# Two routed expert layers behind a short convolution: the first epochs are cut 5 and 2 instead of 7, and the weight addresses of a step are made two to a chunk

## The chip, the cores and the metric

The kernel runs on one core of a Trainium2 chip. The metric is the device time of one execution in microseconds (us). Times of the kernel before are those of three runs and of one profiled execution.

## The reference, cut to what matters

The input x has 4 sequences of 3584 tokens with 192 channels, 14336 tokens in all. Three layers follow one another:

```python
# 1. causal depthwise convolution, 7 taps, softmax of the taps, 8 heads of 24 channels
out = np.einsum('hk,bskhg->bshg', softmax(weight), x_unfolded)
# 2. top-1 experts: 8 experts, 192 -> 1024 -> 192
expert = argmax(x @ w_gate);  p = softmax(x @ w_gate)[expert]
out[n] = p * (relu(x[n] @ w1[expert]) @ w2[expert])
# 3. noisy top-2 experts: 8 experts, 192 -> 1024 -> 192
noisy = x @ w_gate + log1p(exp(x @ w_noise)) * noise
top2 = the two largest of noisy;  q = softmax over the two
out[n] += q_k * (relu(x[n] @ w1[e_k]) @ w2[e_k])      # for both experts
```

## The kernel before

**Units and epochs.** The tokens come in 32 units of 448 (four tiles of 112). `tokens` carries one unit from its load to its scatter: convolution on TensorE (`ph<-x,band`), a split of each value into two halves of 16 bits, transposes, the gate's logits (`pl<-oneoa,rT`), the choice of the expert, a rank within the expert (`rank_mm`, `slots`), and four indirect DMAs from GpSimd (`rows<-row,di`) which put each token's row into the region of its expert in DRAM. `EPOCHS` cuts the 32 units into groups. When a group of units is counted, `epoch_tables` takes a snapshot of the experts' counters, and `table` works out from it, in a chain of small VectorE instructions, which full tiles of 512 or 256 tokens of one expert can be run; what is left goes to the next epoch. The last epoch also has tiles of 128, padded. A unit of epoch k may take its ranks only when k epochs are closed, so that the counters of a snapshot hold exactly the units of its epoch.

**The wait of the first snapshot.** `epoch_tables` begins with one loop that waits both for the counted units and for `ready[0] < 2`. `ready[0]` counts three preparations of the first expert layer's weights: the split of w1 (`first_w1`), the split of w2 (`first_w2`), and the products of w2 with the second gate (`gate_products`). The tables of all epochs go through one lane, one after another.

**Steps.** A tile of T tokens of one expert is a step. `load` reads the tile's place and its expert from the table with two `value_load`s on SyncE, fetches the expert's w1 (`w1t<-w1s`, 1 MB) and the rows, transposed (`xT<-rows`), and a small side table (`ax<-rows`). The DMAs on rows wait for the scatters in `g.deps`, which are all scatters recorded when the epoch was closed. `mm1` makes the hidden layer in 8 chunks of 128 hidden units. A chunk is five matmuls of T columns (`ph<-xT,w1t`); in large steps of the second layer it is four, and half of the small remainder is done for two chunks at once with 64 rows. `mm2` makes the output, three matmuls a chunk and 128 tokens (`py<-w2r,h`). `run` issues the chunks of mm1 of a step alternately with those of mm2 of the step before, so the step before is finished only when the next one has begun.

**Weight addresses.** w2 of all experts is resident in SBUF, and which expert a step uses is known only at run time. `addresses` therefore loads one offset from the table into a register of TensorE (`value_load`) and makes 16 addresses from it with 16 register additions. It is called once in a step, behind the second matmul of the first chunk. TensorE's instructions are read in order, so the matmuls behind it are read after the 16 additions. The four steps that bridge the two layers have w2 of their own (`st.g.own`) and need no addresses.

**Order.** Each engine's order of instructions is fixed when the program is built: a planner (`pump`, `live`, `clk`, `Queue`) runs all the generators against assumed costs and emits whichever instruction is due. The register instructions have no cost in it. `feed` starts the units, with a limit on how many may be under way.

**Two layers.** The first expert layer has 2 steps of 512 tokens, 45 of 256 and 21 of 128; the second has 4 bridge steps of 512, 45 further steps of 512, 7 of 256 and 21 of 128. Rows of the second layer's outputs are added to the result with indirect DMAs (`out_dram<-y,ax`).

Of the kernel before, what the change touches and what calls it, by code (L numbers as in the profile page):

```python
# [13 lines left out]
OP = mybir.AluOpType  # L14
# [5 lines left out]
N, D, E, F = 14336, 192, 8, 1024  # L20
FC = F // P
# [3 lines left out]
NT = SEQ // OT  # L25
G = 4
NG = NT // G
EPOCHS = (7, 4, 3, 4, 4, 4, 6)
DG = D + 2 * E
MAIN = 2 * D  # L30
HALF = MAIN // 2
# [10 lines left out]
NX, NROW, NRT = 4, 4, 3  # L42
# [5 lines left out]
W2_AT = 21472  # L48
# [6 lines left out]
def n_ceil(avail, t):  # L55
    return (avail + E * (t - 1)) // t
# [3 lines left out]
def conv_moe_moe2_kernel(ctx: ExitStack, tc: tile.TileContext, xh, cw, cwb, wg, w11, w21, w2t, w12, w22, out):  # L60
# [64 lines left out]
    v = Queue(nc.vector, "dve", 0.07, 1.04e-3)  # L125
# [11 lines left out]
    def vv():  # L137
        return on("dve", "dve", lat=0.06)

    def poll():  # L140
        return now[0] + 0.25, None

    def spawn(gen, rank=1, at=None):
        live.append([(now[0] if at is None else at, None), gen, rank])
# [196 lines left out]
    s1 = [cst.tile([P, E], F32, name=f"s1_{m}") for m in range(2)]  # L341
    s2 = [cst.tile([P, E], F32, name=f"s2_{m}") for m in range(2)]
    sE = [cst.tile([P, E], F32, name=f"sE_{m}") for m in range(2)]
# [137 lines left out]
    ready = [0, 0]  # L481
# [70 lines left out]
    def second_weights():  # L552
        while done[0] < sum(EPOCHS):
            yield poll()
        open_prep("prep2")
        spawn(second_w1(), 2)
        spawn(second_w2(), 2)
# [73 lines left out]
    def snapshot(m, tag):  # L631

        r = cst.tile([P, E], F32, name=tag + "snap")
        v.tensor_sub(r, cnt[m][cur[m]], reg_e)
        return r
# [99 lines left out]
    flying = [0, 0]  # L735
    done = [0, 0]
# [9 lines left out]

    def tokens(i, epoch):
        b, g = divmod(i, NG)
        wide = epoch == 0 and i % 2
        xs = "y" if wide else "x"  # L750
        yield from take(xs)
        rs = "row0" if wide else "row1"
# [113 lines left out]
    def feed():  # L866
        i = 0
        for k, n in enumerate(EPOCHS):
            for _ in range(n):
                while flying[0] >= (NROW if k else 7) or (k > 1 and ready[0] < 3) or (k and done[0] < EPOCHS[0]):  # L870
                    yield poll()
                flying[0] += 1
                spawn(tokens(i, k), 1 if k == 0 or ready[0] == 3 else 2)
                i += 1
                yield now[0] + 0.5, None

    def pad_rows(m, rows, total):
        pi = cst.tile([P, E], I32, name=f"pi{m}")
        v.scalar_tensor_tensor(pi, total, part, reg_e, op0=OP.add, op1=OP.add)
        yield on("pool", "dve")  # L880
        res = []
        for e in range(E):
            res.append(row_write(m, scatter(rows, pi[:, e:e + 1], pads)))
            yield on("pool")
        return res

    def epoch_tables(k, groups):
        while done[0] < sum(EPOCHS[:k + 1]) or ready[0] < 2:
            yield poll()
        if k == 0:  # L890
            v.tensor_mul(sE[0], s1[0], s2[0])
        total = snapshot(0, f"e{k}")
        closed[0] += 1
        deps = list(scat1)
        put = clk["put"]
        for g in groups:
            if g.last:
                deps = deps + (yield from pad_rows(0, rows1, total))
                put = clk["put"]
            g.deps, g.put = deps, put  # L900
            yield vv()
            yield from table(g, total)
# [34 lines left out]
    def mm1(st, f):  # L937


        T, n = st.T, 512 // st.T  # L940
        if f == 0:
            st.h = wk.tile([P, 2, 512 * FC // n], F16, name="h", tag="h", bufs=2)
            st.hv = st.h.rearrange("p k (c t) -> p k c t", c=FC)
        st.ph = [ps_h.tile([P, 512], F32, name="ph") for _ in range(st.nb)]
        x = lambda k: st.xT[:, k, :]

        def w(b, j, k):
            c = (f + b) * n + j
            return st.w[0][:, k * F + c * P:k * F + (c + 1) * P]

        out_ = lambda b, j: st.ph[b][:, j * T:(j + 1) * T]
        def whole(b):
            for j in range(n):
                o = out_(b, j)
                first = j == 0 and b < 2
                t_.matmul(o, w(b, j, 0), x(0), start=first, stop=False, skip_group_check=True)
                t_.matmul(o, w(b, j, 0), x(2), start=False, stop=False, skip_group_check=True)
                if f == b == j == 0 and not st.g.own:
                    addresses(st)
                t_.matmul(o, w(b, j, 1), x(0), start=False, stop=False, skip_group_check=True)  # L960
                t_.matmul(o, w(b, j, 2), x(1), start=False, stop=b > 1, skip_group_check=True)

        if st.nb == 4:
            whole(0)
            whole(1)
            for b in (0, 2):
                for j in range(n):
                    for i, (rows, src) in enumerate(((slice(0, 64), x(1)), (slice(64, P), st.x3))):
                        t_.matmul(out_(b + i, j), w(b + i, j, 3)[rows], src[rows], start=b == 2 and j == 0,
                                  stop=b == 0, skip_group_check=True)  # L970
            whole(2)
            whole(3)
            return
        for j in range(n):
            o = out_(0, j)
            t_.matmul(o, w(0, j, 0), x(0), start=True, stop=False)
            t_.matmul(o, w(0, j, 0), x(2), start=False, stop=False)
            if f == j == 0 and not st.g.own:
                addresses(st)
            t_.matmul(o, w(0, j, 1), x(0), start=False, stop=False)  # L980
            t_.matmul(o, w(0, j, 2), x(1), start=False, stop=False)
            t_.matmul(o, w(0, j, 3), x(1), start=False, stop=True)
# [12 lines left out]

    w2bytes = w2r.rearrange("p e c -> p (e c)").bitcast(mybir.dt.uint8)

    def addresses(st):

        pe = nc.tensor  # L1000
        first = pe.value_load(st.g.tb[st.i:st.i + 1, 2:3], min_val=0, max_val=4 * (E - 1) * FC * DG)
        step = 2 * (D if st.g.m else DG)
        st.wr = []
        for k in range(2 * FC):
            r = pe.alloc_register(f"w2at{len(addressed)}_{k}")
            pe.reg_alu(r, first, W2_AT + k * step, op=OP.add)
            st.wr.append(pe.snap(r, min_val=W2_AT, max_val=W2_AT + 4 * (E - 1) * FC * DG + k * step,
                                 guaranteed_mod_val=0, out_of_modulus=32))
        addressed.append(st)

    addressed = []

# [226 lines left out]
    def group(m, t, k, last, own, tag):  # L1239

        g = Step()
        g.m, g.t, g.k, g.last, g.own, g.tag, g.tb, g.bc, g.deps = m, t, k, last, own, tag, None, None, None
        g.steps = deque()
        for i in range(k):
            w = [None, None]
            parts_ = []
            for skip in range(0, t, 512):
                st = Step()
                st.g, st.T, st.i, st.skip, st.w, st.first, st.end = g, min(t, 512), i, skip, w, skip == 0, None
                st.nb = 4 if m and t > P else 1  # L1250
                parts_.append(st)
            g.steps.append(parts_)
        return g
# [49 lines left out]
    def full_groups(m, left, sizes, tag):  # L1303
        res = []
        for t in sizes:
            k = n_full(left, t)
            if k:
                left -= k * t
                res.append(group(m, t, k, False, False, f"{tag}{t}"))
        return left, res  # L1310

    left, ep_groups = 0, []
    for k, n in enumerate(EPOCHS):
        left, gs = full_groups(0, left + n * G * OT, (512, 256), f"ta{k}")
        if k == len(EPOCHS) - 1:
            gs.append(group(0, P, n_ceil(left, P), True, False, "ta"))
# [48 lines left out]
    for k, gs in enumerate(ep_groups):  # L1365
        tables.add(epoch_tables(k, gs))
    tables.add(bridge_tables())
    spawn(make_band())
    spawn(gates())
    spawn(feed())  # L1370
    spawn(first_w1(), 1, 0.8)
    spawn(first_w2(), 1, 1.0)
# [67 lines left out]
```

## Time and profile before

| what | value |
|---|---|
| three runs, median (lowest to highest) | 1857.07 us (1856.74 to 1864.67) |
| the profiled execution's own time | 1855.31 us |
| its span, first to last instruction | 1853.4 us |
| TensorE busy in the span | 1689.8 us (91%) |
| VectorE, ScalarE, GpSimd busy | 52%, 46%, 50% |
| mean share of the 16 DMA engines' time | about 70% over the span, all queues |

Matmuls are pipelined and their ends are modelled, so a row's busy time ends a little after the next row's start. Idle time put down to "issue" is time in which the engine waited for nothing that the profile shows. Register instructions, branches and waits on semaphores have no rows; they are seen only by the idle time that they leave. Line 97 stands beside nearly all rows because one helper records every instruction; the names of the tiles tell the rows apart.

### The profile page before, as it was taken

Reading aid. Unit: us, or ns where it says so; the run is one execution under the profiler, and the core shown is the slowest. Engines: PE = TensorE matmul, PEld = TensorE weight load, DVE = VectorE, ACT = ScalarE, POOL = GpSimd, SP = SyncE. Lnnn points to the kernel's source line nnn. Section 1 sums busy time; section 2 is a strip of 40 time slices with the busy share of each in tenths; the row PEclk is TensorE's granted clock in tenths of the full one; section 3 lists DMA queues with packets and bytes.
Section 4 is the critical chain, followed back from the end, with each engine's and each line's share of the span. In section 5 each row is a group of like instructions: output and inputs, shape, how many; then the busy total and the mean of one; then the engine's idle time right before and its main releaser. Section 6 shows DMA issues by size and latency. Waiting matters only on the chain. (4 is left out here: it accounts for less than half of the span.)

```text
span 1853.4 us, 44339 instructions
## 1 busy us (share of the span) xinstructions
PE 1689.8 (91%) x16031; PEld 1327.7 (72%) x16031; DVE 958.9 (52%) x3520; ACT 857.5 (46%) x1756; POOL 921.4 (50%) x1496
## 2 busy tenths in 40 slices
PE   6778788888899888898999999999999999999997
PEld 4548677787888777787566767777677776867766
DVE  8856667576677766565563333333333333343331
ACT  5846556565556555544333333333333333343342
POOL 1553567676766646454865334334333343433334
PEclk7779989899999989899999999999999999999999
DMA  7886676575589898687985457665554867567772
GB/s 301 305 246 217 193 223 182 152 177 163 163 257 297 276 298 253 200 206 226 304 198 107 83 92 135 106 129 108 100 106 79 171 104 161 121 124 168 171 152 27
DMA packets 320215, 328.30 MB, mean 177 GB/s; under 512 B 229630, under 2 KB 277508, under 8 KB 302848
## 3 DMA queue, kind: packets, MB, share of 16 engines
q1 hardware_dynamic: 260048, 243.52, 46.8%
q0 software_dynamic: 53904, 68.63, 19.9%
q10 hardware_dynamic: 6048, 13.32, 2.4%
q8 instruction: 130, 2.13, 0.5%
q14 instruction: 85, 0.70, 0.1%
HBM read 189.50 MB, written 96.08 MB: 154 GB/s over the span
## 5 line engine op out<-in xcount | busy, mean ns | idle before, releaser
L97 PE MATMUL ph<-xT,w1t 128*128 128x256 f16 (+3 forms) x5576 | 838.9, 295 | 67.1 <-issue 52.9
L97 DVE SCALAR_TENSOR_TENSOR h<-ph,h 128x512 f16<-128x512 f32 x700 | 463.2, 687 | 744.6 <-ACT h L97 684.8
L97 PE MATMUL py<-w2r,h 128*128 x8016 | 760.3, 250 | 12.9 <-issue 11.6
L97 PEld LDWEIGHTS <-h 128*128 128x128 f16 x8400 | 722.3, 99 | 66.1 <-issue 31.9
L97 PEld LDWEIGHTS <-w1t 128*128 128x128 f16 (+1 forms) x5800 | 463.1, 99 | 346.8 <-issue 175.4
L97 POOL DMA_INDIRECT out_dram<-y,ax x231 | 358.1, 1550 | 538.7 <-ACT y L97 393.5
L97 ACT ACTIVATE h<-ph 128x512 f16<-128x512 f32 x700 | 403.9, 594 | 444.0 <-PE ph L97 373.8
L97 ACT ACTIVATE y<-py,cf 128x192 f32<-128x192 f32 (+1 forms) x350 | 148.4, 424 | 394.2 <-PE py L97 316.4
L97 POOL DMA_INDIRECT rows<-row,gdi x238 | 237.6, 998 | 130.4 <-issue 45.3
L97 POOL MEMSET spacer<- 128x256 f32 (+1 forms) x613 | 261.4, 426 | 0.2
L97 POOL DMA_INDIRECT rows<-row,di x128 | 129.5, 1012 | 108.5 <-DVE row L97 35.3
L97 PE MATMUL ph<-x,band 118*112 118x96 f32 x512 | 68.0, 297 | 12.9 <-DMA x<-in_xh_dram 11.0
L97 PEld LDWEIGHTS ph<-x,band 118*112 118x112 f32 x512 | 64.2, 210 | 15.0 <-issue 8.7
L97 ACT ACTIVATE x<-x,ras 112x192 f32<-112x192 f32 x128 | 49.1, 445 | 38.6 <-DVE rai L97 22.6
L97 PE MATMUL ph<-x,w1t 64*128 64x512 f16 (+1 forms) x224 | 63.5, 368 | 0.0
L97 ACT ACTIVATE y<-y,rbs 128x192 f32<-128x192 f32 x119 | 47.1, 445 | 5.8 <-DVE rbs L97 3.2
L97 ACT ACTIVATE rT<-ph 128x672 f16<-128x672 f16 x64 | 43.4, 728 | 9.8 <-remote 3.8
L97 DVE TENSOR_TENSOR row<-x,row 112x256 f16<-112x256 f32 x64 | 33.2, 553 | 13.9 <-ACT row L97 13.9
L97 PE MATMUL py<-w2t,h 128*128 128x192 f16 x384 | 35.4, 250 | 3.3 <-issue 3.3
L97 PE MATMUL ph<-ident,row 112*128 112x112 f16 x384 | 28.8, 222 | 9.5 <-DVE row L97 2.9
L97 POOL CAST row<-gix 128x8 f32<-128x8 uint32 (+1 forms) x30 | 7.4, 247 | 60.4 <-DVE gex L97 27.3
L97 PE MATMUL py<-w2tr,gcol 128*32 128x256 f32 x96 | 32.7, 493 | 3.9 <-DVE w2mm L97 3.9
(274 smaller groups left out, 1135.5 us busy)
## 6 DMA issues: line engine op xcount, KB each, us to landing
w1t<-w1s SPq DMA_DIRECT2D x126, 1024.0 KB
x<-in_xh_dram ACTq DMA_DIRECT2D x32, 400.0 KB
w1raw<-in_w_dram SPq DMA_DIRECT2D x8, 1536.0 KB
w2raw<-in_w_dram SPq DMA_DIRECT2D x16, 768.0 KB
out_dram<-pads SPq DMA_DIRECT2D x11, 960.0 KB
w1s<-w1raw POOLq DMA_DIRECT2D x16, 512.0 KB
w1s<-whalf SPq DMA_DIRECT2D x16, 512.0 KB
w2tr<-in_w2t_dram SPq DMA_DIRECT2D x16, 384.0 KB
```

The source lines that it names most:

```text
L97: r = f(*a, **kw)
```

## The change

Three edits stand in the diff. The first epoch has five units and a second epoch of two is put behind it; the limit of the first seven units on load and priority now goes by the number of the unit (`BURST`) and not by its epoch, and later units may start when five units are counted, where it was seven. The snapshot and the closing of an epoch no longer wait for the weights; the table behind them does. `addresses` is called in every chunk and makes two of the 16 addresses there; the load of the offset stays in the first chunk.

```diff
-EPOCHS = (7, 4, 3, 4, 4, 4, 6)
+EPOCHS = (5, 2, 4, 3, 4, 4, 4, 6)
+BURST = 7
@@ tokens
-        wide = epoch == 0 and i % 2
+        wide = i < BURST and i % 2
@@ feed
-                while flying[0] >= (NROW if k else 7) or (k > 1 and ready[0] < 3) or (k and done[0] < EPOCHS[0]):
+                while i >= BURST and (flying[0] >= NROW or (k > 2 and ready[0] < 3) or done[0] < EPOCHS[0]):
                     yield poll()
                 flying[0] += 1
-                spawn(tokens(i, k), 1 if k == 0 or ready[0] == 3 else 2)
+                spawn(tokens(i, k), 1 if i < BURST or ready[0] == 3 else 2)
@@ epoch_tables
-        while done[0] < sum(EPOCHS[:k + 1]) or ready[0] < 2:
+        while done[0] < sum(EPOCHS[:k + 1]):
             yield poll()
-        if k == 0:
-            v.tensor_mul(sE[0], s1[0], s2[0])
         total = snapshot(0, f"e{k}")
         closed[0] += 1
         deps = list(scat1)
         put = clk["put"]
+        while ready[0] < 2:
+            yield poll()
+        if k == 0:
+            v.tensor_mul(sE[0], s1[0], s2[0])
@@ mm1, in both forms of a chunk
                 t_.matmul(o, w(b, j, 0), x(2), start=False, stop=False, skip_group_check=True)
-                if f == b == j == 0 and not st.g.own:
-                    addresses(st)
+                addresses(st, (f + b) * n + j)
@@ addresses
-    def addresses(st):
+    def addresses(st, c):
+        if st.g.own:
+            return
         pe = nc.tensor
-        first = pe.value_load(st.g.tb[st.i:st.i + 1, 2:3], min_val=0, max_val=4 * (E - 1) * FC * DG)
+        if c == 0:
+            st.at2 = pe.value_load(st.g.tb[st.i:st.i + 1, 2:3], min_val=0, max_val=4 * (E - 1) * FC * DG)
+            st.wr = []
+            addressed.append(st)
         step = 2 * (D if st.g.m else DG)
-        st.wr = []
-        for k in range(2 * FC):
+        for k in range(2 * c, 2 * c + 2):
             r = pe.alloc_register(f"w2at{len(addressed)}_{k}")
-            pe.reg_alu(r, first, W2_AT + k * step, op=OP.add)
+            pe.reg_alu(r, st.at2, W2_AT + k * step, op=OP.add)
             st.wr.append(pe.snap(r, min_val=W2_AT, max_val=W2_AT + 4 * (E - 1) * FC * DG + k * step,
                                  guaranteed_mod_val=0, out_of_modulus=32))
-        addressed.append(st)
```

## Rows read from the trace of the kernel before

**Rows 1.** Windows: per stretch the engines' busy time (instructions), granted clock, DMA share, GB/s.
```profile
128.00:300.00 172.00, 142.42 (x1454) 126.73 (x1454) 108.87 (x520) 96.84 (x215) 87.88 (x171) 0.91 0.72 213
300.00:912.00 612.00, 538.71 (x5541) 465.82 (x5538) 402.79 (x1795) 325.26 (x705) 383.31 (x709) 0.96 0.77 223
912.00:1838.00 926.00, 919.52 (x8468) 671.52 (x8467) 347.38 (x791) 352.27 (x676) 387.08 (x496) 1.00 0.64 127
```
**Rows 2.** Groups by line and form, PE: count, busy us, mean ns, idle before, releaser.
```profile
L97 PE MATMUL ph<-xT,w1t 128*128 128x512 f16 x1648 | 396.8, 382 | 1.4 <-issue 1.4
L97 PE MATMUL ph<-xT,w1t 128*128 128x256 f16 x2024 | 273.9, 278 | 45.8 <-issue 32.0 <-DMA xT<-rows 7.5 <-ACT x L97 3.4
L97 PE MATMUL ph<-xT,w1t 128*128 128x128 f16 x1680 | 118.6, 221 | 19.8 <-issue 19.5
```
**Rows 3.** Timeline, PE, 256-token steps: start, us, operation, count, idle before and releaser.
```profile
127.96 0.58 PE L97 MATMUL ph<-xT,w1t 128*128 128x256 f16 x2 [6.78 <-DMA xT<-rows]
129.93 1.86 PE L97 MATMUL ph<-xT,w1t 128*128 128x256 f16 x8 [1.38 <-issue]
...
149.91 1.03 PE L97 MATMUL ph<-xT,w1t 128*128 128x256 f16 x8 [1.38 <-issue]
...
1126.03 1.90 PE L97 MATMUL ph<-xT,w1t 128*128 128x256 f16 x15 [0.16 <-issue]
```
**Rows 4.** Timeline, PE, 128-token steps, the same columns.
```profile
646.72 0.38 PE L97 MATMUL ph<-xT,w1t 128*128 128x128 f16 x4 [1.23 <-issue]
...
1616.77 1.17 PE L97 MATMUL ph<-xT,w1t 128*128 128x128 f16 x18 [0.38 <-issue]
...
1782.13 1.16 PE L97 MATMUL ph<-xT,w1t 128*128 128x128 f16 x18 [0.21 <-issue]
```
**Rows 5.** Timeline, PE, the first two chunks and more of a 512-token step.
```profile
975.91 2.21 PE L97 MATMUL ph<-xT,w1t 128*128 128x512 f16 x9
```
**Rows 6.** Timeline, PE, pace of matmuls of each width, with nothing to wait for.
```profile
152.44 1.26 PE L97 MATMUL ph<-xT,w1t 128*128 128x256 f16 x10
153.53 1.23 PE L97 MATMUL py<-w2r,h 128*128 x12
...
672.04 1.28 PE L97 MATMUL ph<-xT,w1t 128*128 128x128 f16 x20
...
154.74 0.20 PE L97 MATMUL pl<-oneoa,rT 128*112 128x16 f16 x1
...
155.30 0.19 PE L97 MATMUL pl<-oneoa,rT 128*112 128x8 f16 x1
```
**Rows 7.** Timeline, SyncE's queue, around the first step's loads.
```profile
121.17 0.36 SPq L97 DMA_DIRECT2D w1t<-w1s  x1
123.21 1.33 SPq L97 DMA_TRANSPOSE xT<-rows  x1
125.15 0.41 SPq L97 DMA_DIRECT2D ax<-rows  x1
127.08 0.35 SPq L97 DMA_DIRECT2D w1t<-w1s  x1
```
**Rows 8.** Waits of SyncE's queue on the first layer's scatters: us in total, times, longest.
```profile
SPq L97 <- DMA rows<-row,di: 3.9, 2, 2.6
```
**Rows 9.** Timeline, DVE: last split of w2, the first snapshot, the end of its table, what comes next.
```profile
113.40 1.95 DVE L97 SCALAR_TENSOR_TENSOR w2r<-w2raw,w2scs,w2r 128x768 f16<-128x768 f32 x2 [1.03 <-issue]
...
115.34 0.16 DVE L97 TENSOR_TENSOR e0snap<-cnt,reg_e 128x8 f32<-128x8 f32 x1
...
119.58 0.17 DVE L97 COPY ta0256bc<-pr 128x10 f32<-128x10 f32 x1
128.51 0.23 DVE L97 TENSOR_SCALAR cf<-ax,ta0256bc 128x2 f32<-128x2 f32 x1 [8.77 <-DMA ax<-rows]
```
**Rows 10.** Timeline, POOL: the last scatter of the seven units.
```profile
119.56 0.95 POOL L97 DMA_INDIRECT rows<-row,di  x1 [0.17 <-issue]
```
**Rows 11.** Timeline, PE: convolutions of two of the next units.
```profile
132.71 5.77 PE L97 MATMUL ph<-x,band 118*112 118x96 f32 x32
```

## What the change was predicted to do

> **What bounds the kernel now.** I read the windows first, for the stages. From 912 us on TensorE is busy 919.5 of 926 us [rows 1]: there the kernel is as long as TensorE's work, and only a shorter queue of matmuls or the last gaps in it can help. Between 128 and 912 us it is busy 681.1 of 784 us, and no other engine is above 512 us in these two windows [rows 1]. So in the first layer TensorE is the fullest engine too, but 103 us pass there in which it stands.
>
> The groups by form tell where TensorE stands. Before matmuls of mm1 the idle time is 45.8 us for 256 columns and 19.8 us for 128, nearly all "issue", and only 1.4 us for 512 [rows 2]. "Issue" means that no semaphore explains it. The timeline then shows the place: two matmuls of a step run, a gap comes, and the remaining 8 (or 18) of the row follow [rows 3, 4]. That is exactly where `addresses` stands. I counted the gaps of this pattern over the whole timeline: 40 in steps of 256 columns (26.7 us; the first is at 129.93 us, the last at 1126.03 us), 32 in steps of 128 (12.7 us; first 646.72, last 1782.13) and one of 1.4 us with 512 columns, together 40.8 us. By stage it is 7.1 us before 300 us, 27.8 us from there to 912 us and 5.9 us in the last stage.
>
> **What one call of `addresses` costs.** The first step has just waited for its rows, so nothing had been read ahead: from its first matmul to the third 1.97 us pass [rows 3]. Two pairs of weight load and matmul cost about 0.1 us to issue (below), so a load and 16 additions take 1.87 us. At 149.91 the visible gap is 1.38 us again [rows 3]; the usual gap is smaller because matmuls already queued run meanwhile. A step of 512 columns shows nine matmuls in 2.21 us with no gap in them [rows 5], so register instructions don't drain the array: they only hold back what is read next.
>
> How the 1.87 us split between load and additions decides what is saved, and TensorE's trace has no row for it. The nearest row is SyncE's: from the end of the `ax` DMA at 125.56 to the next w1 DMA at 127.08 are 1.52 us [rows 7], in which it does two such loads and some address arithmetic. One load is then at most about 0.75 us; 16 additions take 1.12 us, one 0.07 us, and the 14 that leave the first chunk 0.98 us. The bounds: if the load took all of SyncE's 1.52 us, 14 additions are 0.31 us; if it took nothing, 1.64 us. I take 0.98 us, since one load of two is what the row holds. A gap can give back no more than its own length, so each of the 73 counts with the smaller of its length and 0.98 us: 23.1 us of the 256-column steps (6.3 before 300 us, 16.6 to 912, 0.2 later), 1.0 of the 512-column one, 11.9 of the 128-column steps (6.1 to 912 us, 5.8 later). At 0.31 us these are 12.1, 0.3 and 8.8; at 1.64 us 26.3, 1.4 and 12.7.
>
> **Where the additions go, and what hides them.** Each later chunk gets two additions, 0.14 us. A 256-column chunk runs at (1.26 - 0.28)/9 = 0.109 us a matmul, from its row and the group's mean of one [rows 2, 6]; the logits show 12 matmuls of 8 and 16 columns started in 0.56 us, 0.051 us each [rows 6], so issuing a pair takes no longer than that. Five matmuls leave 5 x 0.058 = 0.29 us, more than 0.14: hidden, without any lead. At 512 columns it is wider still. At 128 columns the pace is (1.28 - 0.22)/19 = 0.056 us [rows 2, 6], which leaves 0.02 us in a chunk: not hidden there. What covers it is mm2, which stands between: 12 matmuls at 0.089 us [rows 6] give 0.46 us of lead. Over a whole narrow step, 40 matmuls of mm1 and 24 of mm2 take 4.4 us on the array, and issuing takes 64 x 0.051 + 1.87 = 5.1 us at most, whatever the order. So in runs of narrow steps spreading can save nothing, or, if a pair issues faster than 0.051 us, nearly all of 11.9 us. I take half, 6.0 us: 3.05 to 912 us, 2.9 later.
>
> [...]
>
> [...]
>
> **How much of it the end sees.** In the last stage, all of it. From 300 to 912 us TensorE is busy 88% [rows 1], and its other stops are waits on chains that start from TensorE; I take nine tenths of 16.6 + 1.0 + 3.05 = 20.7, so 18.6 us. Before 300 us the units' chain (load, split, rank, scatter, table) sets the pace and TensorE is busy 83% [rows 1]: half of 6.3, 3.1 us. Last stage: 2.9 + 0.2 = 3.1 us. Sum 24.8 us.
>
> **The epochs.** First step. VectorE's last split of w2 ends at 115.35 us and the snapshot and table follow at once, to 119.75 [rows 9]. So the weights set the table's start, and taking the snapshot earlier brings the table forward by a few tenths at most. What does move: the first step's rows no longer wait for the sixth and seventh unit. SyncE issued w1 by 121.53 but the transposes at 123.21 [rows 7], and its queue waited 3.9 us on scatters, two times [rows 8]; the seventh unit's last scatter was made at 119.56 to 120.51 [rows 10]. Gain: 1.68 us less an issue gap of a tenth or two, 1.5 us. Each of these loads is on SyncE's queue in order, so the `ax` table and the next w1 move up with it.
>
> By the tiling's arithmetic 5 units give 1 step of 256 and 2 more give 4, where 7 gave 5: the steps are the same, but the second waits for a second table. That table costs one more chain like that from 115.53 to 119.75, some 4.2 us of VectorE, in a place where VectorE stood 8.77 us waiting for `ax` [rows 9]; if the planner emits it behind that wait, it ends near 127 + 4 = 131 us, and its step's data, 7 us after (119.75 to 127.96 less the 1.5 us) [rows 3, 9], near 138 us. The second step began at about 148 us before, its gap being at 149.91 [rows 3]: hidden by 10 us. Uncovered it would cost the excess. The sixth and seventh unit wait for a snapshot that now needs five units only; their scatters may come 1 to 2 us later, hidden by the same 10 us. Units from the eighth on start at five counted units, so their convolutions, 5.8 us of them at 132.71 [rows 11], can move into the 6.8 us in which TensorE waited [rows 3]. Between -8 and +5 us in all; since the units' chain sets the pace up to 300 us, I take 2 us gained, the 1.5 us and a little.
>
> **Sum.** 24.8 + 2 = 26.8 us. The profiled execution took 1855.31 us (span 1853.4): 1828.5 us. The median of the runs is 1.8 us above it: 1830 us.
>
> **Rivals.** *The load is the price.* The gaps stay at 0.7 of their size because the load stays. For it: no row of TensorE tells load from additions. Against: SyncE's two loads in 1.52 us [rows 7]. Price: 12.1 + 0.3 us, nothing of the narrow steps, nine tenths realized: 11 us, 1846 us. Chance 0.15, two thirds of it beyond 0.5%.
>
> *The additions come back in every chunk* (slower). If a register addition holds the array itself, the place is chunks 2 to 8 of the 45 + 42 narrower steps: 87 x 7 x 0.14 = 85 us, less 36 saved, 1906 us. It decides from 36/(87 x 7) = 0.059 us a chunk. For it: the narrow chunks have only 0.02 us to spare. Against: the nine matmuls without a gap [rows 5] and the 0.29 us to spare in the 256-column chunks. Chance 0.06.
>
> *The wait takes another place.* TensorE reaches its next semaphore sooner and waits there, since rows, tables and units' loads come no earlier. For it: 7.5 us on rows and 3.4 us on ScalarE stand in its list already [rows 2]. Against: GpSimd, VectorE and ScalarE are at 53 to 66% [rows 1]. Price: all gains before 912 us, so 1855 - 3 = 1852 us and with the median 1853 us. Chance 0.07.
>
> *The second epoch is late.* The second table is emitted behind the sixth and seventh unit's scatters and the step behind it; the head loses 10 to 15 us and the rest gains: 1842 to 1850 us. Against: the 10 us of slack. Chance 0.10, a third of it still beyond 0.5% faster.
>
> **How the numbers follow.** The forecast (1815 to 1842 us) has 0.62. Half a per cent of 1857 is 9.3 us, about what a measurement of this kernel tells from no change, so faster means below 1848. Faster: 0.62 + 0.10 + 0.03 = 0.75. Same: 0.05 + 0.07 + 0.06 = 0.18. Slower: 0.06 and 0.01 of the late epoch, 0.07. The range goes down to 1812, where every gap gives all 40.8 us and the head some more, and up to 1848, which takes in the load as the price.
>
> **What the profile after would show.** Right: the idle time in front of mm1 at 256 columns falls from 45.8 to below 25 us and the gap behind the second matmul is mostly gone; the first row fetch follows w1's DMA within 0.3 us; a second snapshot and table lie near 120 to 131 us, and the second step starts by 148 us; the last stage is 2 to 5 us shorter. Wrong: gaps remain there at nearly full size (the load), new "issue" gaps between the chunks of narrow steps (the additions), or as much new waiting on DMA, ScalarE or VectorE before 912 us.

## The result, and the profile after

The kernel after takes 1811.64 us (median of 4 runs, 1805.37 to 1815.0) against 1856.9 us (4 runs, 1851.63 to 1864.67): a ratio of 0.9757, 95% interval 0.9725 to 0.9788, 45 us. The forecast was 1830 us, 27 us less than before, and its range went down to 1812 us: this median lies 0.4 us outside it. The profiled execution took 1815.0 us (span 1813.2), 40 us less than that of before.

The windows after (columns as in [rows 1]). The last two edges are moved so that the last window holds as many TensorE matmuls as before, 8469 and 8468:

```profile
129.00:300.00 171.00, 150.88 (x1520) 135.09 (x1521) 116.09 (x587) 97.46 (x215) 98.78 (x197) 0.90 0.80 225
300.00:884.00 584.00, 523.67 (x5447) 454.39 (x5447) 389.71 (x1739) 317.98 (x692) 382.71 (x693) 0.97 0.78 229
884.00:1798.00 914.00, 914.00 (x8469) 671.27 (x8470) 347.06 (x791) 352.35 (x676) 385.57 (x492) 1.00 0.66 130
```

TensorE's idle time before 912 us was 103 us in [rows 1]; up to 884 us it is now 80 us, and the last window is 12 us shorter. The groups by form, the same as in [rows 2]:

```profile
L98 PE MATMUL ph<-xT,w1t 128*128 128x512 f16 x1648 | 392.6, 380 | 3.1 <-DVE h L98 2.4 <-DMA xT<-rows 0.7
L98 PE MATMUL ph<-xT,w1t 128*128 128x256 f16 x2024 | 273.6, 279 | 23.5 <-issue 13.5 <-DMA xT<-rows 6.3 <-DVE h L98 1.2
L98 PE MATMUL ph<-xT,w1t 128*128 128x128 f16 x1680 | 113.9, 222 | 7.1 <-issue 6.6
```

Before the 256-column matmuls 23.5 us are left of 45.8, before the 128-column ones 7.1 of 19.8. Counted over the timeline, the gaps behind the second matmul of a step went from 73 with 40.8 us to 25 with 10.6 us. The first step, and a run of 128-column steps late in the kernel:

```profile
129.27 0.59 PE L98 MATMUL ph<-xT,w1t 128*128 128x256 f16 x2 [6.33 <-DMA xT<-rows]
130.37 1.87 PE L98 MATMUL ph<-xT,w1t 128*128 128x256 f16 x8 [0.51 <-issue]
...
1574.57 1.28 PE L98 MATMUL ph<-xT,w1t 128*128 128x128 f16 x20
1576.67 1.28 PE L98 MATMUL ph<-xT,w1t 128*128 128x128 f16 x20
```

The gap of 1.38 us [rows 3] is 0.51 us, so 14 additions took 0.87 us, 0.062 us each.

The register instructions have rows after all, against what was said above: the timeline leaves them out, but the view of one source line (`--source`) gives their count, shortest, median and longest time in ns, and the first and last start. Here are the load and the additions of the first step before, where the 16 additions stand as five instructions, and then all additions of the kernel after, one instruction a chunk:

```profile
L1001 PEldq TENSOR_LOAD <-ta0256tb x1: 495/495/495, 128.0 to 128.0; - x1
L1006 PEldq FUSED_REGOPS  x3: 105/160/186, 128.9 to 129.8; - x3
L1007 PEldq FUSED_REGOPS  x2: 163/163/163, 129.1 to 129.6; - x2
```
```profile
L1011 PEldq FUSED_REGOPS  x1128: 105/105/131, 130.2 to 1786.3; - x188
```

From 128.9 to the end of the last instruction at 129.9 the 16 additions take 1.0 us, 0.063 us each. Counted over the whole trace of before, the median call takes 0.70 us from the start of the load to the first addition and 1.70 us in all.

In the last stage the 20 matmuls now stand in one row: the gaps of [rows 4] are gone. But the first step is not earlier. It begins at 129.27 us where it began at 127.96 [rows 3]. VectorE's timeline shows the snapshot taken early and the table, as before, behind the split of w2:

```profile
106.61 0.16 DVE L98 TENSOR_TENSOR e0snap<-cnt,reg_e 128x8 f32<-128x8 f32 x1
...
113.38 1.95 DVE L98 SCALAR_TENSOR_TENSOR w2r<-w2raw,w2scs,w2r 128x768 f16<-128x768 f32 x2 [0.75 <-ACT w2r L98]
116.30 0.22 DVE L98 TENSOR_TENSOR tbav<-e0snap,used 128x8 f32<-128x8 f32 x1
```

SyncE's wait for the scatters did go. These are its semaphore instructions between the first step's table and its transposes, before and after; the longest, which ends with a scatter (`rows<-row,di`) before, falls from 1.21 to 0.03 us:

```profile
L97 SPq EVENT_SEMAPHORE  x9: 13/28/1214, 120.9 to 123.1; - x9
L98 SPq EVENT_SEMAPHORE  x9: 3/13/28, 121.1 to 123.3; - x9
```

But w1 is issued at 121.90 us where it was 121.17 [rows 7], and the transposes at 123.37 where they were 123.21: between the two, SyncE's instructions pause once for 0.68 us with no wait that the profile knows.

ScalarE's queue shows what else moved: the loads of the eighth to eleventh unit, before and then after.

```profile
113.32 0.33 ACTq L97 DMA_DIRECT2D x<-in_xh_dram  x1
116.66 1.30 ACTq L97 DMA_DIRECT2D x<-in_xh_dram  x3
```
```profile
105.20 0.33 ACTq L98 DMA_DIRECT2D x<-in_xh_dram  x1
105.57 0.46 ACTq L98 DMA_DIRECT2D x<-in_xh_dram  x1
113.03 0.34 ACTq L98 DMA_DIRECT2D x<-in_xh_dram  x1
119.17 0.34 ACTq L98 DMA_DIRECT2D x<-in_xh_dram  x1
```

### The profile page after: what moved, and what is told of

It is laid out like the page before. It is cut to its first block, busy times and chain, and to the rows that moved or that the text cites. A ratio compares the mean times of both kernels' runs of the same rounds, so it can differ in the third digit from the quotient of the medians.

```text
span 1813.2 us, 44787 instructions
## 1 busy us (share of the span) xinstructions
PE 1680.4 (93%) x16033; PEld 1326.3 (73%) x16033; DVE 957.2 (53%) x3547; ACT 856.9 (47%) x1756; POOL 929.3 (51%) x1496
## 5 line engine op out<-in xcount | busy, mean ns | idle before, releaser
L98 PE MATMUL ph<-xT,w1t 128*128 128x256 f16 (+3 forms) x5576 | 830.0, 295 | 33.6 <-issue 20.1
L98 POOL DMA_INDIRECT rows<-row,gdi x238 | 242.6, 1019 | 87.5 <-issue 57.3
L98 POOL DMA_INDIRECT rows<-row,di x128 | 129.3, 1010 | 101.8 <-ACT y L98 33.4
L98 PEld LDWEIGHTS <-row 112*128 112x128 f16 x384 | 25.3, 108 | 18.1 <-issue 13.1
```

What stands on the lines that cost most here:

```text
L98: r = f(*a, **kw)
```

## The experiments

All ratios are to the kernel before, timed beside it on the same chip. Runs e1 to e4 were on a chip where the kernel before takes 1861 us; e5 to e8, e9 to e12 and e13 to e18 were on three others, where it takes 1789 to 1795 us. So only ratios, or times of one chip, are compared. On which chip the first result and the profile of the kernel before (1855 us) were taken is not on record; their times are those of the slower one, and they are compared with e1 to e4.

**e1, the addresses alone.** Of the change's diff only `addresses` and its two calls. The instructions of all engines but the register ones stand in the order of before.

> The kernel before with the addresses made two by two and nothing else; the epochs stay 7, 4, 3 and so on. Theory A (the gap behind the second matmul cost more than its idle time shows, since the modelled end of the matmul ahead of it hides some 0.17 us of each; the epochs are worth next to nothing): 37 to 43 us faster than before, ratio 0.977 to 0.980, and the last stage, where no epoch is left, is about 12 us shorter. Theory B (the addresses are worth what the visible gaps give, 30 us, and the new epochs the rest): 26 to 32 us faster, ratio 0.983 to 0.986.

0.9859 (0.9827 to 0.9891), 26 us: theory B's number. A's total is refuted, but what it said of the last stage, some 12 us shorter, came true (below). The forecast had put the addresses at 24.8 us.

**e2, the epochs alone.** The other half: `EPOCHS`, `BURST`, `feed`, `epoch_tables`; 16 addresses at once. Here too the order is exactly that of the kernel after.

> The kernel after with the 16 addresses made at once in the first chunk, as before: only the epochs, the closing without the weights and the units' start differ from before. Theory A: within 4 us of before, ratio 0.998 to 1.002, the first step's first matmul within 2 us of 128 us. Theory B: 10 to 16 us faster, ratio 0.991 to 0.995.

0.9865 (0.9831 to 0.9898), 25 us: more than either theory had said. The first step starts at 130.1 us, so nothing is gained there, and yet the epochs give as much as the addresses. Where, is looked for by cutting the timelines at the starts of the same rows:

| us (profiled execution) | before | after | e1 | e2 |
|---|---|---|---|---|
| first matmul of mm1 | 128.0 | 129.3 | 129.5 | 130.1 |
| from there to the last convolution | 340.0 | 315.3 | 331.1 | 312.6 |
| to the first 64-row matmul (bridge) | 418.2 | 416.2 | 410.5 | 420.3 |
| to the last mm2 of the bridge | 77.7 | 75.2 | 77.0 | 71.9 |
| to the last matmul | 878.9 | 866.5 | 866.5 | 878.6 |

The addresses give 8.9, 7.7 and 0.7 us in the first layer and 12.4 us in the last stage. With the epochs alone the stretch in which units are still fed is 27 us shorter. Not all of that is gained: other matmuls stand ahead of the last convolution. The windows of these two stretches, before and then e2:

```profile
127.96:467.96 340.00, 288.12 (x3000) 257.16 (x2999) 224.48 (x1116) 197.48 (x442) 206.79 (x402) 0.94 0.66 191
467.96:963.84 495.88, 444.89 (x4429) 370.29 (x4426) 317.22 (x1321) 244.81 (x518) 300.34 (x530) 0.96 0.84 244
```
```profile
130.11:442.73 312.62, 272.59 (x2878) 244.33 (x2879) 215.07 (x1097) 189.35 (x422) 202.93 (x398) 0.95 0.72 198
442.73:934.91 492.18, 445.52 (x4520) 375.70 (x4517) 322.94 (x1378) 244.56 (x520) 316.00 (x543) 0.98 0.85 252
```

In e2 122 fewer matmuls lie in the first stretch and 91 more in the second. Over both, e2 is 31 us shorter. TensorE's idle time falls by 16 us of that, from 102.9 to 86.7; the other 15 us are shorter busy time, with 31 matmuls fewer of 7429. In the traces of before and after the granted clock is 1.00 or 0.50 at any time (40 and 42 stretches). If it has these two levels in e2 as well, TensorE was at the lower one, by the means above, for about 80 us before and 51 us in e2 (within 8 us, as the means have two digits). From start to start a 256-column matmul took 0.213 us at 0.50 and 0.109 us at 1.00 (medians of before; eight of the first step, at 0.50, take 1.86 us and eight at 149.91, at 1.00, take 1.03 us [rows 3]). So, as an estimate from these numbers, up to 14 us, half of the difference, come from the clock. No run separates how much of that the early start brings and how much differs from one execution to the next: the kernel after, with the same order as e2, has 70 us at the lower level between the same rows. The group of the convolutions in e2:

```profile
L98 PE MATMUL ph<-x,band 118*112 118x96 f32 x512 | 67.2, 292 | 2.8 <-DMA x<-in_xh_dram 1.9 <-DVE band L98 0.6
```

and in the kernel before:

```profile
L97 PE MATMUL ph<-x,band 118*112 118x96 f32 x512 | 68.0, 297 | 12.9 <-DMA x<-in_xh_dram 11.0 <-DVE h L97 0.8 <-DVE band L97 0.6
```

**e3 and e4, the price of a load and of an addition.**

```diff
+        again = pe.value_load(st.g.tb[st.i:st.i + 1, 2:3], ...)      # e3: odd addresses are made from it
...
-        for k in range(2 * FC):
+        for k in range(3 * FC):                                      # e4: mm2's third matmul has its own
```

> The kernel before with a second load of the same offset behind the first in every call; odd addresses are made from the second. Theory of the forecast (a load takes about 0.75 us, the rest of the 1.87 us is the additions): every exposed call loses 0.7 to 0.8 us more, with 75 to 95 calls exposed 50 to 75 us slower, and the first step's visible gap grows from 1.38 us to about 2.15 us. If the load is the price (1.5 us): 110 us slower or more, gap about 2.9 us. If the additions are nearly all of it (load under 0.3 us): under 25 us slower.

> The kernel before with 24 additions in every call in place of 16: the third matmul of each output chunk has an address of its own, with the same value. At 0.065 us an addition: 0.5 us more in every exposed call, 33 to 45 us slower, the first step's gap about 1.8 to 1.9 us. If the load is the price: under 12 us slower, gap about 1.5 us. If the additions cost 0.11 us each: 65 us or more, gap about 2.3 us.

e3: 1.0365 (1.0332 to 1.0398), 68 us slower; e4: 1.0211 (1.0178 to 1.0244), 39 us slower. Both lie in the interval that the forecast's split of the 1.87 us gave. The first step's gap, in e3 and then in e4:

```profile
132.52 1.87 PE L97 MATMUL ph<-xT,w1t 128*128 128x256 f16 x8 [2.09 <-issue]
```
```profile
132.33 1.86 PE L97 MATMUL ph<-xT,w1t 128*128 128x256 f16 x8 [1.85 <-issue]
```

Against 1.38 us [rows 3] a load costs 0.71 us and eight additions 0.47 us, 0.059 each. In e3 the 512-column steps, which hid one call whole [rows 5], show it too:

```profile
1008.10 0.61 PE L97 MATMUL ph<-xT,w1t 128*128 128x512 f16 x2
1009.23 1.77 PE L97 MATMUL ph<-xT,w1t 128*128 128x512 f16 x7 [0.53 <-issue]
```

**e5 and e6, which part of the epochs.** e5 is one number in the kernel before; e6 is e2 with the later units' start put back to seven.

```diff
-  ... or (k and done[0] < EPOCHS[0])):
+  ... or (k and done[0] < 5)):          # e5, on before (EPOCHS[0] is 7)
-  ... or done[0] < EPOCHS[0]):
+  ... or done[0] < BURST):              # e6, on e2 (EPOCHS[0] is 5, BURST 7)
```

> The kernel before with one number changed: units from the eighth on may start when five units are counted instead of seven. Epochs, tables, the wait for the weights and the addresses are those of before. Theory F (the new epochs gain by this start: loads of x are issued near 105 us instead of 113 to 117 us and TensorE no longer waits 11 us for them): 15 to 25 us faster than before, ratio 0.987 to 0.992. Theory S (the split into 5 and 2 gains by itself): within 6 us. Theory L (any other order of the planner moves the time by this much): no statement.

> Epochs of 5 and 2 and the closing without the weights, as in the kernel after, but units from the eighth on wait for seven counted units as before, and the addresses are made at once as before. Theory F: at most 8 us faster than before, ratio 0.996 or more. Theory S: 15 to 25 us faster.

e5: 0.992 (0.9904 to 0.9937), 14 us, with the epochs untouched; F had said 15 to 25 us. e6: 0.9975 (0.9955 to 0.9995), 4 us. By these two the start gives it, and not the split (theory F), if the order alone (theory L) does not.

**e7 and e8, two edits without a purpose.** Planned times of 0.5 us (between two starts of units) and 12 us (between the DMAs that zero the output) become 0.6 and 13 us.

> The kernel before with 0.6 instead of 0.5 planned us between two starts of units: it does the same work and has no purpose, but the planner's order comes out another way from then on. Theories F and S: within 6 us of before. Theory L: 10 us or more away from before, to either side.

> The kernel before with 13 instead of 12 planned us between the DMAs that zero the output: the same work, no purpose, another order of the planner from the first step on. Theories F and S: within 6 us of before. Theory L: 10 us or more away from before, to either side.

0.9945 (0.9921 to 0.9969) and 0.9961 (0.994 to 0.9981): 10 and 7 us faster, for nothing. So the planner's order alone moves the time by some 5 us to either side of a middle, and the order of before is the slowest of the four with a start at seven. F could not be told from L by e5 alone: its interval and that of e7 overlap.

**e9 to e12, on one chip.** e9 is the kernel after, e10 is e2 again, e11 is e5 with the addresses two by two. e12 is the kernel after with the load one step earlier:

```diff
+    def offset(st):
+        st.at2 = nc.tensor.value_load(st.g.tb[st.i:st.i + 1, 2:3], ...)
...
                     mm2(prev, f * pairs // ns, (f + nb) * pairs // ns)
+                    if st is not None and f == ns - nb and n + 1 < len(seq):
+                        nx = seq[n + 1].g
+                        if not nx.own and nx.tb is not None and now[0] >= nx.ready:
+                            offset(seq[n + 1])
```

> The kernel after, unchanged, timed beside the next three on one chip. Whatever the chip, about 2 to 2.5 per cent faster than before if both halves of the change hold there (ratio 0.975 to 0.981); about 1.2 to 1.7 per cent (0.983 to 0.988) if what the epochs gave depends on the stalls in which TensorE's instructions come late, and this chip has few of those.

> The epochs with the addresses made at once, a second time. On a chip whose first layer shows some 20 us or more of idle time put down to issue elsewhere than behind the second matmul of a step: 1.0 to 1.6 per cent faster, as at first. On a chip without such idle time: theory F or S 0.7 to 1.2 per cent faster; theory L (the order before is merely a poor one among many) about what the two neutral edits gave, 0.2 to 0.7 per cent.

> The kernel before with two edits: the addresses two by two, and units from the eighth on started at five counted units; the first epoch stays 7. Theory F: no slower than the kernel after, ratio to before 0.972 to 0.982. Theory S (the split is needed): at least 8 us slower than the kernel after, ratio 0.982 or more.

> The kernel after with the load of the offset moved as well: for nearly every step it is issued one step earlier, right behind the last matmuls of mm2, instead of behind the second matmul of its first chunk; the additions stay, and every engine's other instructions keep their order. If the load is what is left of the gaps (25 gaps, 10.6 us visible in the profile after): 5 to 15 us faster than the kernel after, and those gaps nearly gone. If the load only moves its stall with it: within 4 us of the kernel after.

e9: 0.9731 (0.9692 to 0.977), faster than both of its expectations. e10: 0.9882 (0.9841 to 0.9922), 21 us. e11: 0.9739 (0.9697 to 0.9781), as fast as the kernel after with the first epoch still at seven, so the split is not needed. e12: 0.9707 (0.9665 to 0.975), 1741.05 against 1743.91 us: within 4 us of the kernel after. The "issue" gaps of its load fall from 4.3 to 0.5 us in the two groups below, and ahead of the 128-column matmuls the waits on rows rise by 2.1 us. First e9, then e12:

```profile
L98 PE MATMUL ph<-xT,w1t 128*128 128x256 f16 x2024 | 260.0, 276 | 10.9 <-DMA xT<-rows 6.6 <-issue 3.0 <-DVE h L98 0.7
L98 PE MATMUL ph<-xT,w1t 128*128 128x128 f16 x1680 | 109.0, 220 | 5.7 <-DMA xT<-rows 4.4 <-issue 1.3
```
```profile
L98 PE MATMUL ph<-xT,w1t 128*128 128x256 f16 x2024 | 262.0, 279 | 6.0 <-DMA xT<-rows 4.2 <-DVE h L98 0.8 <-issue 0.5
L98 PE MATMUL ph<-xT,w1t 128*128 128x128 f16 x1680 | 108.5, 220 | 6.5 <-DMA xT<-rows 6.5
```

**e13 to e16, start or luck.** The start at four and at six on the kernel before, and e5 with each of the two purposeless edits.

> The kernel before with the eighth unit's start at four counted units instead of seven, nothing else. Theory F, with the start as a dose: as fast as at five or up to 6 us faster, ratio 0.986 to 0.993. Theory L: anywhere between 0.990 and 1.003, without order along 7, 6, 5, 4.

> The kernel before with the eighth unit's start at six counted units instead of seven. Theory F: between seven and five, ratio 0.993 to 0.998. Theory L: as for four.

> Start at five counted units, and the neutral 0.6 us between two starts of units besides. Theory F: ratio to before 0.983 to 0.993, and at least 5 us faster than the same neutral edit without the early start (0.9945). Theory L: its distance to before has nothing to do with the start; 0.993 to 1.000 as likely as below.

> Start at five counted units, and the neutral 13 us between the DMAs that zero the output besides. Theory F: ratio 0.983 to 0.993, at least 5 us faster than that neutral edit without the early start (0.9961). Theory L: 0.993 to 1.000 as likely as below.

All orders with the addresses at once on the three chips where the kernel before takes 1789 or 1790 us, by the later units' start. e5 to e8 were on the first of them, e10 on the second, e13 to e16 on the third:

| start at | ratios to before | mean |
|---|---|---|
| seven | 1, 0.9945 (e7), 0.9961 (e8), 0.9975 (e6) | 0.9970 |
| four to six | 0.992 (e5), 0.9882 (e10), 0.9885 (e13), 0.9823 (e14), 0.9875 (e15), 0.9888 (e16) | 0.9879 |

The groups don't overlap: an early start is worth 0.9%, 16 us. One reserve stays: all orders with a start at seven were on the first chip, and all but one of the early ones on the other two. The ratio of one kernel differs by 0.002 to 0.003 between chips (e2 and e10, e9 and e18), less than the 0.009 here. Within each group the order moves the time by up to 10 us either way, and the dose has no order: six is the fastest, faster than F had said (0.993 to 0.998), and five as in e5 the slowest. So F holds for the group, and L for the differences inside it.

**e17 and e18, the version that the runs point to.** Start at six, addresses two by two and the load ahead, with epochs of 7, 4, 3 (e17), beside the kernel after (e18).

> The version that the runs point to: the kernel before with three edits, the later units' start at six counted units (e14), the addresses two by two, and the load of the offset one step ahead (e12). The epochs stay 7, 4, 3. If the gains add: 0.982 times 0.984 times 0.998, about 0.965 of before and 12 to 20 us faster than the kernel after. If TensorE's other waits take over what the addresses give: within 6 us of the kernel after.

> The kernel after, unchanged, on the chip of the run before it, for a comparison of the two: ratio to the kernel before 0.970 to 0.978.

e17: 0.9675 (0.9644 to 0.9707), 1738.15 us; e18: 0.9701 (0.9675 to 0.9728), 1740.44 us. It beats the kernel before, but not clearly the kernel after: 2 us between the medians, where 12 to 20 us were expected if the gains add. TensorE's longest waits of e17 are on rows, the gate's preparation and x.

```profile
PE ph L97 <- DMA xT<-rows: 13.6, 8, 5.6
PE py L97 <- DVE gwm L97: 10.5, 1, 10.5
PE ph L97 <- DMA x<-in_xh_dram: 9.1, 5, 3.2
```

## Why the prediction was right and wrong

**The addresses: the mechanism right, the sum partly by luck.** A load "at most about 0.75 us" measured 0.71 (e3), an addition at 0.07 us measured 0.059 (e4) and 0.062 (after), and the sum of 24.8 us measured 26 us (e1). "TensorE's trace has no row for it" was wrong: the rows of line 1001 and of the additions, above, hold this split already in the trace of before, at 0.70 and 1.0 us, and no bounds from SyncE's loads were needed. The two additions of a chunk are one instruction of 0.105 us, where 0.14 us was taken. The rival *the load is the price* is refuted by e3 and e4, and the rival *the additions come back in every chunk* by e1: its 256- and 128-column groups hold 12.5 and 8.4 us of issue time where [rows 2] have 32.0 and 19.5:

```profile
L97 PE MATMUL ph<-xT,w1t 128*128 128x256 f16 x2024 | 268.9, 278 | 26.8 <-issue 12.5 <-DMA xT<-rows 9.3 <-ACT row L97 1.8
L97 PE MATMUL ph<-xT,w1t 128*128 128x128 f16 x1680 | 114.9, 221 | 9.1 <-issue 8.4
```

**Its parts were mis-sized, both ways.** The last stage was to give 3.1 us and gave 12.4. The step that failed here is "A gap can give back no more than its own length". A row's busy time ends with a modelled end: one matmul of 128 columns is drawn 0.221 us long [rows 2] where the pace is 0.056 us [rows 6], so every gap behind one is drawn 0.165 us too short. The timeline of before shows it:

```profile
1606.90 0.28 PE L97 MATMUL ph<-xT,w1t 128*128 128x128 f16 x2
1607.35 1.17 PE L97 MATMUL ph<-xT,w1t 128*128 128x128 f16 x18 [0.17 <-issue]
...
1620.87 2.35 PE L97 MATMUL ph<-xT,w1t 128*128 128x512 f16 x9
```

The third matmul starts 0.45 us after the first, where two take 0.11: 0.34 us lost, 0.17 drawn as idle. And the row of nine 512-column matmuls is 2.35 us long where [rows 5] have 2.21, with no gap drawn at all. In the last stage 22 drawn gaps hold 5.9 us and their tails 22 x 0.165 = 3.6 us. Before and e1 have the same order of matmuls, so their starts can be compared one by one: the matmuls behind the 22 gaps give 9.5 us, and third matmuls of 256 and 512 columns, which no drawn gap precedes, give 2.7 us. The half that was taken off for narrow steps was wrong as well: their gaps in that stage are all gone.

In the first layer the addresses were to give 21.7 us and gave 8.9 + 7.7 + 0.7 = 17.3 us (e1). Compared one by one in the same way, the third matmuls of its steps give 33.8 us there, and 16.6 us are lost again elsewhere. Of these, 4.4 us are waits on semaphores; between the last convolution and the end of the bridge they rose from 7.7 to 14.4 us. That is the rival *the wait takes another place*, in part. The other 12 us are "issue" gaps and time with no drawn gap, and from one execution of each kernel they can't be told from chance. So one error, the tails left out, made up for another, too little taken off for what is lost elsewhere.

**The epochs: wrong, and this put the time outside the range.** The step that failed is "Between -8 and +5 us in all; since the units' chain sets the pace up to 300 us, I take 2 us gained". They gave 25 us on the slower chip (e2) and 21 us on a faster one (e10). The 1.5 us at the first step did not come: the wait on the scatters went, as argued, but SyncE's later start and its pause took it up. (Of the 3.9 us in [rows 8] only 1.2 us stood there; the other wait is at 517.8 us.) The second table is hidden as argued (in the kernel after, the second step is under way at 143.55 us). What was priced too low is the early start. It was counted as 5.8 us of convolutions that can fill a hole; but it puts the loads of two units 8 to 11 us earlier, and the chain behind them (convolution, split, rank, scatter, table), which was named as what sets the pace, was then not moved. e5, e6 and e13 to e16 show that the start is worth 16 us, with the reserve on chips above.

Through what it acts is not settled. On the slower chip the last convolution of e2 ends 25 us sooner than before, and TensorE's wait for x falls from 11.0 to 1.9 us. On the faster ones the waits for x are no shorter: 2.6 to 5.0 us with a start at seven (e6 to e8), 0 to 11.8 us with an early one. There the first layer, from the first matmul of mm1 to the last row of the bridge, takes 757.5 us on the mean of e6 to e8 and 744.5 us on that of the six early orders. Only 4.5 of the 13 us are idle time; the rest is busy time. The granted clock, on the mean of the stretch up to the last convolution and of that behind it, was 0.94 to 0.95 and 0.98 to 0.99 with the late start, 0.94 to 0.97 and 0.98 to 1.00 with the early one; at the levels 1.00 and 0.50 this puts TensorE at the lower one for 46 us and 37 us, an estimate from means of two digits. A shorter time at the lower level is thus likely a part of the gain, and the forecast had no term for it.

The rest of the 21 to 25 us, 5 to 9 us, fits the order: an edit without a purpose moved the time by 7 or 10 us, and the order of before was a poor one. No term of the forecast allowed for that, so its bounds for the epochs were too narrow.

## What to carry to other kernels

Register work on TensorE was paid here only as far as it outlasted what was queued ahead of it: in the first step, behind two matmuls, a call of 1.9 us left a gap of 1.38 us [rows 3], and in the 512-column step of [rows 5] none. Cut such work into pieces no longer than what the next few matmuls leave over (here 0.105 us a chunk), and look up its rows by the source line before its price is guessed. Read a gap of pipelined matmuls from start to start, less the pace, and not from the drawn idle time (above, 0.34 us lost and 0.17 drawn). Where a planner or any other chaotic order fixes the schedule, time two or three edits without a purpose first (here they moved the time by 10 and 7 us); a difference below their spread says nothing. And do not price an edit that starts the chain which sets the pace by the first hole that it can fill: here that gave 2 us, and the early start was worth 16.

## What the runs showed of the hardware

The kernel before takes 1861 us on one chip and 1789 to 1795 us on three others, some 4% less. e2 and e10 are one program, 1832 and 1769 us; its first layer, from the first matmul of mm1 to the end of the bridge, takes 804.8 us on the one and 742.1 us on the other, its last stage 878.6 and 878.9. The idle time before mm2 tells one part, e2 first:

```profile
L98 PE MATMUL py<-w2r,h 128*128 x8016 | 757.0, 250 | 12.1 <-issue 10.0 <-DVE h L98 0.4 <-ACT h L98 0.2
```
```profile
L98 PE MATMUL py<-w2r,h 128*128 x8016 | 745.3, 249 | 1.0 <-DVE h L98 1.0
```

In e10 no "issue" is listed there, where e2 has 10.0 us. In the profile of the kernel before, whose times are those of the slower chip, one or two matmuls start every 0.7 to 0.8 us over stretches of some microseconds, with no wait that the profile knows. SyncE's pause of 0.68 us in the kernel after is of about the same length. This timeline is of the kernel before:

```profile
902.74 0.24 PE L97 MATMUL py<-w2t,h 128*128 128x192 f16 x1 [0.38 <-issue]
903.54 0.33 PE L97 MATMUL py<-w2t,h 128*128 128x192 f16 x2 [0.57 <-issue]
904.28 0.24 PE L97 MATMUL py<-w2t,h 128*128 128x192 f16 x1 [0.41 <-issue]
```

Their cause was not tried.

How far TensorE runs ahead can be read from the call of e3 whose gap ends at 1009.23 us, above. Its first load starts at 1006.8 us, while the row of mm2 ahead of it still runs:

```profile
L1001 PEldq TENSOR_LOAD <-tb1024tb x1: 300/300/300, 1006.8 to 1006.8; - x1
```
```profile
1003.97 4.12 PE L97 MATMUL py<-w2r,h 128*128 x48
1007.93 0.34 PE L97 MATMUL pr<-tbdg,ones 128*128 128x42 f32 x2
```

At (4.12 - 0.25)/47 = 0.082 us a matmul, 13 or 14 of mm2 have not yet started; with the two of the next row and the first two of the step some 17 matmuls are queued ahead. Counted over all calls of the kernel before, from the start of the load to the second matmul of the step, 110 of 141 have exactly 17, and none has more. So a call of 1.7 us is hidden where 17 matmuls take as long: 15 of mm2 and two of 512 columns (0.216 us from start to start) take 15 x 0.082 + 2 x 0.216 = 1.66 us.
